# XCiT attention and a GELU MLP on one core: a rearranged start, the last stores in a fixed order, a fourth output buffer, six more Strassen sets and a new step order

## The chip, the core and the metric

The kernel runs on one core of a Trainium2 chip. Five engines work side by side, each through its own instructions in their written order: TensorE (PE in the profile; its weight loads are PEld), VectorE (DVE), ScalarE (ACT), GpSimd (POOL) and SyncE (SP). SP, ACT and POOL also issue DMA transfers. The metric is the device time of one execution in microseconds (us). Before the change the median of three runs is 684.43 us (683.51 to 684.55).

## The reference

For each of 4 batches, q, k and v are 6080 x 256. The columns of q and k are normalised over the tokens, a 256 x 256 attention matrix is taken over the channels, and v times that matrix goes through a two-layer MLP of width 2048:

```python
qn = q / (np.linalg.norm(q, axis=1, keepdims=True) + 1e-06)
kn = k / (np.linalg.norm(k, axis=1, keepdims=True) + 1e-06)
s = kn.transpose(0, 2, 1) @ qn / tau
a = np.exp(s - s.max(-1, keepdims=True)); a /= a.sum(-1, keepdims=True) + 1e-09
x = (v @ a).reshape(24320, 256)
h = x @ w_in
g = 0.5 * h * (1.0 + np.tanh(c * (h + 0.044715 * h * h * h)))
out = g @ w_out
```

## The kernel before

The kernel never forms `v @ a`. For each batch it computes `aw = a @ w_in` (256 x 2048, in four slices of 512 columns) and then `h` straight from the transposed tokens `vT` and `aw`. The tokens are cut into 25 blocks: 0 to 5, 6 to 11 and 12 to 17 belong to the first three batches (five blocks of 1024 tokens and one of 960 each), 18 to 24 to the last (five of 1024, one of 512, one of 448; block 24 is `LAST`).

Start (batch 0). The chunks of q and k are loaded by DMA; for each, `early_squares` squares q on ACT and k on DVE, `gram_row` adds k against q into the bank `G` (two matmuls of 256 columns a row), and `ss_rows` sums the squares through matmuls with ones (`SS[1]` for k, 256 columns wide; `SS[0]` for q, one column). The first four chunks are folded on DVE from eight rows to four (`early_fold`), the last two are not. The last chunk arrives in five pieces. `warm` issues matmuls on zeros. `scores` then takes roots by `Ln` and `Exp` on ACT (`lnk`, `rk`, `lnq`, `rq`), scales `G` on DVE into `S`, and takes the exponentials into `eT` (two halves). `pe_vt` transposes the first 512 tokens on PE and `pe_vt_copy` copies them to `vT`. `first_aw` sums the rows of `eT`, takes the reciprocal `rs` and makes the first slice of `aw` in four pieces, three copied on DVE and one on ACT. After that the first product of the MLP can run.

Body. All steps of all blocks stand in one text, `ORDER`, whose words are run in turn; so the text fixes the order on each engine. A word names a step, its part, the PSUM bank it opens (`@a` to `@g`, and `@z`) and the block or batch. The first product of the MLP comes in two forms. A plain step (`g.u_x`, then `G.u_x`) is two 512-column matmuls and a GELU on ACT. A set replaces four plain steps by seven products (`m1` to `m7`) after Strassen and Winograd, with two copies on ACT (`wcq`, `wy5`; `Y5_DVE` may send the second to DVE), two additions on DVE (`wap`, `wax`) and four GELUs (`wGp`, `wGs`, `wGr`, `wGx`). A full block has seven sets and four plain steps; blocks 0, 1, 2, 6, 7, 8, 12, 13 and 14 have fewer sets, 150 in all. The second product uses the same scheme for blocks 0 to 23 (`M1` to `M7` with token sums `T1` to `T4`). `T3`, which `M7` reads, is done for blocks 1 to 22 by an accumulating DMA issued on POOL (`token_sum`). Block 24 uses plain products (`D`, in `direct`), each over all channels of both output halves, into one bank for each half of the tokens.

While a batch runs, the next one's q and k are loaded, squared, folded and summed, so DVE and ACT have work of two kinds. Each result bank is turned by a DVE transpose into an output buffer `ot` (pool `yout`, three buffers), of which `store` issues four DMA stores, on SP. For block 24 the words `sB` and `sA` place the stores of its two halves within the order, alternating SP and ACT. In the built program the transfers issued by SP and ACT count their landing on eight counters in turn.

Of the kernel before, what the change touches and what calls it, by code (L numbers as in the profile page):

```python
# [16 lines left out]
def kernel(  # L17
# [46 lines left out]
    yout = ctx.enter_context(tc.tile_pool(name="yout", bufs=3))  # L64
# [180 lines left out]

    def ss_rows(c, which, rows=None):
# [28 lines left out]
    def scores(b):  # L275
        lnk = smx.tile([128, 256], FP32, tag="lnk")
        nc.scalar.activation(lnk, SS[1], AF.Ln, bias=eps)
        rk = smx.tile([128, 256], FP32, tag="rk")
        nc.scalar.activation(rk, lnk, AF.Exp, scale=-0.5)
        lnq = smx.tile([128, 2], FP32, tag="lnq")  # L280
        nc.scalar.activation(lnq, SS[0], AF.Ln, bias=eps)
        rq = smx.tile([128, 2], FP32, tag="rq")
        nc.scalar.activation(rq, lnq, AF.Exp, scale=-0.5, bias=log_it)
        S = smx.tile([128, 2, 256], FP32, tag="S")
        eT = smx.tile([128, 2, 256], BF16, tag="eT")
        for jc in range(2):
            nc.vector.tensor_mul(S[:, jc, :], G[b][:, jc, :], rk)
        for jc in range(2):
            nc.scalar.activation(eT[:, jc, :], S[:, jc, :], AF.Exp, scale=rq[:, jc : jc + 1])
        ET[b] = eT  # L290
# [15 lines left out]
    def k_row(b):  # L306
        rr, rh = NRM[b]
        dg = smx.tile([128, 256], FP32, tag="lnk", name=f"dg{b}")
# [155 lines left out]
    def pe_vt_copy(n, h, cc):  # L464
        x, y = parts_of(n)[h]
        nc.vector.tensor_copy(vt_tile(n)[:, cc, x:y], VPS[n, h][:, cc, :])
# [218 lines left out]
    def token_sum(n, i, h):  # L685

        hc = hc_of(n)
        if i == 3:
            o = quarter(n, 0, 1, h)
        else:  # L690
            o = tp.tile([128, 4, 512], BF16, tag="tx" if i in (1, 4) else "ty", name=f"t{i}{h}_{n}")[:, :, :hc]
        TS[n, i, h] = o
        if i == 3 and n in SUMS_DMA:
# [34 lines left out]
    def direct(n, p, t, tag):  # L728

        hc = hc_of(n)  # L730
        for m in range(2):
            first = (n, t) not in ACC
            if first:
                ACC[n, t] = bank(tag, [128, 512], f"o{n}_{t}")
                BITS[tag] = 2 * hc
            for fc in (2 * p, 2 * p + 1):
                w = ((A11, A12), (A21, A22))[m][fc // 8]
                mm(ACC[n, t][:, m * hc : m * hc + hc], lhsT=wcomb[:, w, fc % 8, :],
# [3 lines left out]
    XS, CS, OT, TURNED = {}, {}, {}, {}  # L742
# [11 lines left out]
    def store(n, tj, engines):  # L754
# [5 lines left out]
        for bi in range(4):  # L760
            engines[bi].dma_start(
                out=dst[bi],
                in_=ot[bi * 32 : bi * 32 + 32, 0 : hc // 32].rearrange("p x h c -> p x (h c)"))

    def mm2_step(n, what, tag):
# [13 lines left out]
        elif what in ("sA", "sB"):  # L779
            store(n, 1 if what == "sA" else 0, (nc.sync, nc.scalar, nc.sync, nc.scalar))  # L780
        else:
            ci, tj = {"c22": (1, 1), "c11": (0, 0), "c12": (0, 1), "c21": (1, 0)}[what]
            if n == LAST:
                src = ACC[n, tj][:, ci * hc : ci * hc + hc]
# [6 lines left out]
    with tc.manual_schedule():  # L791
# [29 lines left out]
        for c in range(nch - 1):  # L821
# [41 lines left out]
        warm(8)  # L863
# [3 lines left out]
        pe_vt_copy(0, 0, 1)  # L867
# [72 lines left out]


# [11 lines left out]
Y5_DVE = {}  # L953
# [3 lines left out]
g.3_0@f:0 g.0_0@g:0 g.2_0@a:0 aw.2@b:0 aw.3@c:0 ac.2:0 ac.3:0 g.1_0@d:0 vp.1@z:0 vc.1_1:0 vc.1_0:0  # L957
g.7_0@e:0 aw.5@b:0 ac.5:0 G.7_0:0 aw.4@c:0 G.2_0:0 g.5_0@e:0 ac.4:0 aw.7@a:0 ac.7:0 lk.0:1 g.4_0@b:0
G.1_0:0 G.0_0:0 G.5_0:0 G.3_0:0 g.3_1@d:0 G.3_1:0 g.10_1@g:0 g.2_1@c:0 aw.6@e:0 g.9_0@a:0 g.1_1@f:0
lk.1:1 SW.0:0 g.4_1@d:0 G.4_0:0 G.10_1:0 G.9_0:0 g.5_1@b:0 pA21:0 G.2_1:0 ac.6:0 g.14_1@g:0 G.1_1:0  # L960
vp.0@z:1 g.12_1@e:0 g.11_1@a:0 g.10_0@c:0 pA11:0 pS3:0 vc.0_0:1 G.5_1:0 g.6_1@f:0 G.11_1:0 G.4_1:0
G.14_1:0 G.10_0:0 g.8_0@b:0 G.12_1:0 lq.0:1 g.0_1@a:0 g.9_1@d:0 g.15_1@g:0 g.6_0@c:0 g.8_1@e:0
G.0_1:0 G.9_1:0 pF0:0 g.7_1@a:0 lv.1:1 G.6_0:0 G.6_1:0 G.8_1:0 vc.0_1:1 g.13_1@d:0 G.7_1:0 G.13_1:0
pS1:0 SW.1:0 pF1:0 T1.1:0 T1.0:0 pS4:0 M1.1@c:0 g.3_0@f:1 G.15_1:0 g.4_0@e:1 pNA:0 G.4_0:1 lq.1:1
g.15_0@a:0 G.3_0:1 g.12_0@d:1 g.0_0@g:1 M1.0:0 g.11_0@e:0 G.8_0:0 lt.1:1 T2.0:0 g.10_0@f:1 T3.1:0
pA12:0 G.11_0:0 G.12_0:1 G.10_0:1 ksq.0:1 M5.1@b:0 M5.0:0 lv.0:2 y5:0 G.15_0:0 qsq.0:1 row.0_2@z:1
T2.1:0 g.13_0@e:0 f1.0:1 row.0_1:1 row.0_4:1 g.2_0@d:1 g.14_0@f:0 m1.1@b:1 G.0_0:1 G.2_0:1 pS2:0
f2.0:1 vs:1 lq.2:1 g.12_0@a:0 f3.0:1 T3.0:0 g.8_0@g:1 G.14_0:0 G.12_0:0 wcq.1@d:1 row.0_3:1 G.8_0:1
# [12 lines left out]
m5.3@e:2 m2.3:2 G.0_0:2 row.2_5:1 y5:1 T2.0:1 wy5.3:2 G.4_0:2 wy5.1:2 row.2_2:1 m1.1@f:2 m6.3:2
T3.1:1 g.12_0@a:2 row.3_5:1 g.8_1@e:2 row.2_1:1 row.3_0:1 wap.3@c:2 wcq.1@b:2 m6.1:2 row.3_4:1
G.8_1:2 lq.5:1 wap.1@e:2 G.12_0:2 m2.1:2 wGp.3:2 f2.3:1 m7.3:2 row.3_3:1 m3.3:2 wax.3:2 row.2_4:1
M1.0@a:1 m5.2@g:2 m3.1:2 m7.1:2 M1.1:1 gc:1 wGs.3:2 f3.3:1 T4.0:1 lv.1:3 m1.5@c:2 sp.3@z:1 m4.3:2
wGx.3:2 wGp.1:2 wy5.2:2 wGs.1:2 g.12_1@b:2 T3.0:1 wax.1:2 cq@g:1 ksq.4:1 qsq.4:1 m4.1:2 M2.1:1
wGr.3:2 wcq.5@e:2 G.12_1:2 wGr.1:2 m1.2@d:2 m2.5:2 wcq.2@b:2 M2.0:1 m5.5@f:2 lq.6:1 sa.3:1 f1.4:1
m6.2:2 m2.2:2 wGp.5:2 m1.6@e:2 M6.0:1 m6.5:2 wy5.5:2 wcq.6@f:2 lk.6:1 c11:1 wGp.2:2 f2.4:1 wap.2@a:2
T4.1:1 m3.2:2 m7.2:2 m2.6:2 wGx.1:2 wax.2:2 g.0_1@b:2 M6.1:1 wGs.2:2 m4.2:2 wGp.6:2 G.0_1:2
wap.5@a:2 f3.4:1 m6.6:2 ap@f:1 c22:0 wGr.2:2 wGx.2:2 m5.6@b:2 m3.5:2 lt.0:3 sp.4@z:1 ksq.5:1 m7.5:2
m1.7@d:2 M7.1:1 wax.5:2 qsq.5:1 f1.5:1 sa.4:1 f2.5:1 lt.1:3 M3.1:1 M7.0:1 m4.5:2 wGs.5:2 wcq.7@a:2  # L990
wy5.6:2 M3.0:1 m6.7:2 ax:1 m5.7@b:2 f3.5:1 wGr.5:2 wy5.7:2 m2.7:2 sp.5@z:1 M4.0:1 wGx.5:2 wap.6@c:2
sa.5:1 m7.6:2 wap.7@b:2 wax.6:2 qsq.6:1 wGp.7:2 row.4_2@z:1 row.4_3:1 m3.7:2 m7.7:2 c12:1 ksq.6:1
# [342 lines left out]
```

## Time and profile before

| | us |
|---|---|
| median of three runs | 684.43 (683.51 to 684.55) |
| the profiled execution's own time | 684.09 |
| its span in the trace | 682.3 |
| first product of the MLP starts | 38.23 |
| last matmul ends | 675.7 |
| last transpose of the output ends | 676.5 |

The page gives busy time and share for each engine, the span in 40 slices, and the chain of work that ended last, followed back from the end. Start times are counted from the start of the span. A row of the timeline reads: start, duration, engine, line, operation, output and inputs, shapes, count, and in brackets the idle time before it and what ended it. Rows of groups end in total busy time, mean nanoseconds of one, idle time before, and its causes. Matmuls overlap, so a matmul's duration in a row is longer than the time until the next one starts. ACTq, SPq and POOLq are the issuing sides of those engines.

### The profile page before, as it was taken

The page shows a single profiled execution, that of the slowest core. Times are in us where ns is not written, and L with a number is a line of the kernel's source. Part 1 is how long each engine was busy: PE and PEld are TensorE (multiplying, and loading weights), DVE is VectorE, ACT ScalarE, POOL GpSimd, SP SyncE. Part 2 cuts the span into 40 slices and gives each one's busy share as a digit, 9 for nine tenths or more (in the row PEclk, how much of TensorE's full clock was granted, in tenths as well). Part 3 has the DMA queues.
Part 4 walks back from the last instruction along what each step waited for, and adds up shares of the span by engine and source line. Part 5 has one row for each costly group of instructions (what it writes and reads, how often), then busy time and mean ns, then how long its engine had stood idle before and what let it go on. Part 6 is the DMA issues. An engine that isn't in the chain of part 4 may idle for free.

```text
span 682.3 us, 10610 instructions
## 1 busy us (share of the span) xinstructions
PE 663.0 (97%) x3579; PEld 336.3 (49%) x3579; DVE 612.2 (90%) x941; ACT 621.5 (91%) x1193; POOL 112.4 (16%) x177
## 2 busy tenths in 40 slices
PE   3999999999999999999999999999999999999996
PEld 2855455454445454554444444545444444444575
DVE  3579999999998999999999999989998988888893
ACT  5379999899999998999989999999999999999982
POOL 4321121121120121103101111202011011101100
PEclk9999999999999999999999999999999999999999
DMA  9998999998989999959779999878386587558445
GB/s 240 208 256 126 151 180 167 178 165 136 175 151 175 171 164 155 175 80 166 129 135 169 175 167 197 134 134 150 69 148 115 101 151 147 101 107 152 81 84 96
DMA packets 168807, 101.70 MB, mean 149 GB/s; under 512 B 150240, under 2 KB 153952, under 8 KB 168032
## 3 DMA queue, kind: packets, MB, share of 16 engines
q0 software_dynamic: 20688, 62.34, 53.2%
q1 hardware_dynamic: 146816, 37.41, 29.6%
q10 hardware_dynamic: 1248, 1.28, 0.6%
q8 instruction: 28, 0.46, 0.3%
q14 instruction: 27, 0.22, 0.1%
HBM read 78.91 MB, written 36.57 MB: 169 GB/s over the span
## 4 chain that ended last, share of the span: by engine, by line
PE 93%; DMA 3%; DVE 2%; ACT 0%; issue 0%; SPq 0%; POOL 0%; DVEq 0%; POOLq 0%
PE rb L481 18%; PE p L481 17%; PE q L481 15%; PE r L481 11%; PE h L481 10%; PE m L481 10%; PE G L205 6%; PE awp L375 2%; DMA qk_f<-in_q_dram 1%; DMA g<-g 1%; PE o L481 1%; PE warm L269 1%; PE ss L263 1%; DVE t L700 0%; DMA vT<-vb 0%; DVE q L622 0%
## 5 line engine op out<-in xcount | busy, mean ns | idle before, releaser
L481 PEld LDWEIGHTS <-wcomb 128*128 128x128 bf16 x1408 | 136.6, 98 | 144.9 <-issue 3.4
L631 ACT ACTIVATE g<-q 128x512 bf16<-128x512 f32 (+1 forms) x286 | 169.4, 623 | 5.7 <-PE q L481 5.1
L481 PEld LDWEIGHTS <-aw 128*128 128x128 bf16 x807 | 77.9, 98 | 77.1 <-DVE aw L415 1.3
L622 DVE TENSOR_TENSOR q<-rb,yw 128x512 f32<-128x512 f32 (+2 forms) x150 | 102.4, 687 | 13.3 <-PE rb L481 4.4
L700 DVE TENSOR_TENSOR t<-g,t 128x2048 bf16<-128x2048 bf16 (+2 forms) x96 | 112.7, 1180 | 0.1
L625 DVE TENSOR_TENSOR xw<-rb,yw 128x512 f32<-128x512 f32 (+2 forms) x150 | 101.5, 678 | 10.1 <-PE rb L481 7.5
L481 PE MATMUL rb<-tv,sw 128*128 128x512 bf16 (+3 forms) x314 | 109.2, 367 | 0.0
L539 ACT ACTIVATE g<-h 128x512 bf16<-128x512 f32 (+1 forms) x164 | 97.1, 650 | 5.3 <-PE h L481 5.1
L619 ACT ACTIVATE yw<-m 128x512 f32<-128x512 f32 (+2 forms) x150 | 93.0, 626 | 3.9 <-PE m L481 2.9
L481 PE MATMUL p<-t,wcomb 128*128 128x512 bf16 (+2 forms) x384 | 95.5, 373 | 0.0
L631 ACT ACTIVATE g<-xw 128x512 bf16<-128x512 f32 (+1 forms) x143 | 92.6, 650 | 2.7 <-DVE xw L625 2.3
L613 ACT ACTIVATE q<-rb 128x512 f32<-128x512 f32 (+2 forms) x150 | 90.6, 614 | 4.7 <-PE rb L481 3.0
L481 PE MATMUL r<-g,wcomb 128*128 128x512 bf16 (+2 forms) x384 | 94.7, 373 | 0.0
L481 PE MATMUL h<-vT,aw 128*128 128x512 bf16 (+2 forms) x336 | 93.5, 377 | 0.8 <-DVE aw L415 0.8
L481 PEld LDWEIGHTS <-sw 128*128 128x128 bf16 x628 | 61.2, 98 | 61.8 <-issue 1.2
L631 ACT ACTIVATE g<-rb 128x512 bf16<-128x512 f32 (+1 forms) x143 | 87.7, 619 | 2.5 <-PE rb L481 2.1
L694 POOL DMA_DIRECT2D g<-g x44 | 39.7, 917 | 196.3 <-ACT g L631 92.0
L700 DVE TENSOR_TENSOR t<-g 128x2048 bf16<-128x2048 bf16 (+2 forms) x48 | 56.4, 1184 | 1.6 <-ACT g L539 1.3
L481 PE MATMUL q<-vT,sw 128*128 128x512 bf16 (+3 forms) x157 | 56.2, 367 | 0.0
L481 PE MATMUL q<-vT,aw 128*128 128x512 bf16 (+3 forms) x157 | 55.8, 367 | 0.0
L481 PE MATMUL rb<-vT,aw 128*128 128x512 bf16 (+3 forms) x157 | 55.7, 367 | 0.0
L481 PE MATMUL m<-tv,sw 128*128 128x512 bf16 (+3 forms) x157 | 55.7, 367 | 0.0
(148 smaller groups left out, 858.4 us busy)
## 6 DMA issues: line engine op xcount, KB each, us to landing
out_dram<-ot SPq DMA_DIRECT2D x160, 128.0 KB, 4.3
g<-g POOLq DMA_DIRECT2D x38, 512.0 KB, 6.4
vb<-in_v_dram POOLq DMA_DIRECT2D x38, 256.0 KB, 5.2
k<-in_k_dram POOLq DMA_DIRECT2D x21, 384.0 KB, 5.6
q<-in_q_dram POOLq DMA_DIRECT2D x21, 384.0 KB, 5.8
g<-g POOLq DMA_DIRECT2D x6, 480.0 KB, 6.6
out_dram<-ot SPq DMA_DIRECT2D x24, 120.0 KB, 7.5
wst<-in_moe_w_out_dram POOLq DMA_DIRECT2D x2, 1024.0 KB, 10.4
```

The costliest lines, as they stand in the source:

```text
L205: nc.tensor.matmul(G[b][:, jc, :], lhsT=qt[:np_, r, jc * 128 : jc * 128 + 128], rhs=kt[:np_, r, :], start=first and jc == 0, stop=jc == 1, ...
L263: nc.tensor.matmul(SS[1], lhsT=ones_bf, rhs=sq[:, 256:512], start=c == 0 and r == 0, stop=end)
L375: nc.tensor.matmul(ps, lhsT=ET[b][:, jc, ic * 128 : ic * 128 + 128], rhs=win_bf[:, jc, fs * 512 : fs * 512 + 512], start=jc == 0, stop=jc ...
L481: GATE[0] = nc.tensor.matmul(*a, skip_group_check=True, **kw)
L539: nc.scalar.activation(g_half(n, u // 8)[:, x, u % 8], hp[:, :hc], AF.Gelu_apprx_tanh)
L613: nc.scalar.activation(Q[n, i, 0][:, :w], RB[n, i][:, :w], AF.Copy)
L619: nc.scalar.activation(YW[n, i][:, :w], M5.pop((n, i))[:, :w], AF.Copy)
L622: nc.vector.tensor_add(Q[n, i, 1][:, :w], RB[n, i][:, :w], YW[n, i][:, :w])
L625: nc.vector.tensor_add(XW[n, i][:, :w], RB[n, i][:, :w], YW.pop((n, i))[:, :w])
L631: nc.scalar.activation(g[:, t, k0], x[:, :w], AF.Gelu_apprx_tanh)
L694: nc.gpsimd.dma_start(out=o, in_=quarter(n, 1, 1, h), accum_op=ALU.add)
L700: (nc.vector.tensor_add if add else nc.vector.tensor_sub)(o, a, b)
```

## The change

The start is rearranged. The squares of k in the fifth chunk are folded on DVE (`early_fold_k`), as are two pairs of rows of q in the last chunk, so `ss_rows` sums four rows of k and two rows of q fewer. The last sums of q stand ahead of the last row of `G`. `warm(8)` becomes `warm(6)`. One of the two copies into `vT` goes to ACT.

Blocks 6, 7, 8, 12, 13 and 14 get a seventh set in place of four plain steps (156 sets in all, and 24 plain steps fewer). In blocks 18 to 22 two of the seven `y5` copies go to DVE. The whole `ORDER` is new, 3994 words for 3946.

In block 24 the second token half accumulates its two output halves in separate banks (`D.p_1_m`), so that 16 words become 24 for the same matmuls. The words `sA` and `sB` are gone: both halves are stored behind all steps, ACT and SP alternating, and a dependence that only fixes the order ties each store to the one before it. The pool `yout` has four buffers; `lnk`, `rk` and `dg` share the buffers of `dn` and `th`. A DMA form of `T2` is added to the code, for no block (`SUMS2_DMA` is empty).

In all, PE has 16 matmuls fewer: six of 512 columns in the body, and at the start six of 256 columns and four of one. DVE has 25 instructions more.

```diff
-    yout = ctx.enter_context(tc.tile_pool(name="yout", bufs=3))
+    yout = ctx.enter_context(tc.tile_pool(name="yout", bufs=4))
...
+    def early_fold_k(c):
+        k = [x[:, :, 256:512] for x in SQ[c]]
+        nc.vector.tensor_add(k[0], k[0], k[1])
...
-        lnk = smx.tile([128, 256], FP32, tag="lnk")
+        lnk = smx.tile([128, 256], FP32, tag="dn", name="lnk")
...
-    def pe_vt_copy(n, h, cc):
+    def pe_vt_copy(n, h, cc, eng="dve"):
         x, y = parts_of(n)[h]
-        nc.vector.tensor_copy(vt_tile(n)[:, cc, x:y], VPS[n, h][:, cc, :])
+        o, i = vt_tile(n)[:, cc, x:y], VPS[n, h][:, cc, :]
+        if eng == "act":
+            nc.scalar.activation(o, i, AF.Copy)
+        else:
+            nc.vector.tensor_copy(o, i)
...
-    def direct(n, p, t, tag):
+    def direct(n, p, t, *mt):
...
+        *ms, tag = mt
+        key = (n, t, *ms)
+        for m in ms or range(2):
+            first = key not in ACC
...
         for bi in range(4):
-            engines[bi].dma_start(
+            inst = engines[bi].dma_start(
                 out=dst[bi],
                 in_=ot[bi * 32 : bi * 32 + 32, 0 : hc // 32].rearrange("p x h c -> p x (h c)"))
+            if n == LAST:
+                tc.add_manual_dep(inst.ins, STORED[-1].ins.name, mybir.DependencyInfo(
+                    mybir.DependencyClass.NoSync, mybir.DependencyReason.SCHED_ONLY), reason="order")
+            STORED.append(inst)
...
-        elif what in ("sA", "sB"):
-            store(n, 1 if what == "sA" else 0, (nc.sync, nc.scalar, nc.sync, nc.scalar))
...
             if c < nch - 2:
                 early_fold(c)
+            else:
+                early_fold_k(c)
...
-        ss_rows(c - 1, 1)
+        ss_rows(c - 1, 1, range(0, 4))
         ss_rows(c - 1, 0)
         early_squares(c, 0, 0, 4, "act")
+        nc.vector.tensor_add(SQ[c][0][:, 0:2, 0:256], SQ[c][0][:, 0:2, 0:256], SQ[c][0][:, 2:4, 0:256])
         early_squares(c, 1, 0, 5, "dve")
         for i in range(4):
             gram_row(0, c, i)
-        ss_rows(c, 0, range(0, 4))
+        early_squares(c, 1, 5, 8, "dve")
         ss_rows(c, 1, range(0, 5))
-        early_squares(c, 1, 5, 8, "dve")
+        ss_rows(c, 1, range(5, 8))
         early_squares(c, 0, 4, 6, "dve")
-        ss_rows(c, 1, range(5, 8))
         for i in (4, 5):
             gram_row(0, c, i)
-        ss_rows(c, 0, range(4, 6))
+        ss_rows(c, 0, (0, 1, 4, 5))
         early_squares(c, 0, 6, 8, "dve")
-        for i in (6, 7):
-            gram_row(0, c, i)
-        ss_rows(c, 0, range(6, 8))
+        gram_row(0, c, 6)
+        ss_rows(c, 0, (6, 7))
+        gram_row(0, c, 7)
...
-        warm(8)
+        warm(6)
         pe_vt(0, 0, "e")
         scores(0)
         pe_vt_copy(0, 0, 0)
-        pe_vt_copy(0, 0, 1)
+        pe_vt_copy(0, 0, 1, "act")
...
+    for tj in range(2):
+        store(LAST, tj, (nc.scalar, nc.sync) * 2)
...
-Y5_DVE = {}
+Y5_DVE = {(18, 2), (18, 5), (19, 2), (19, 5), (20, 2), (20, 5), (21, 2), (21, 5), (22, 2), (22, 5)}
...
 ORDER = """
...
-D.2_0:24 wGx.3:24 wGr.2:24 D.6_1:24 D.0_0:24 wGs.2:24 D.7_0:24 D.1_0:24 D.6_0:24 D.2_1:24 D.5_1:24
-D.7_1:24 c11:24 c21:24 c12:24 sB:24 c22:24 sA:24
...
+D.0_1_1@d:24 D.5_1_1:24 D.1_0:24 m4.3:24 wGp.3:24 wGr.3:24 D.2_0:24 c21:23 D.3_0:24 c22:23 D.6_0:24
+wGx.3:24 wGx.2:24 D.7_0:24 D.7_1_0:24 c11:24 c21:24 D.1_1_1:24 D.2_1_0:24 D.5_1_0:24 wGs.3:24
+D.4_1_1:24 D.6_1_1:24 D.1_1_0:24 D.4_1_0:24 D.6_1_0:24 D.2_1_1:24 D.3_1_0:24 D.7_1_1:24 D.3_1_1:24
+c12:24 c22:24
```

More of the change, by code (lines that the diff above doesn't have):

```diff
@@ L307, in k_row @@
         rr, rh = NRM[b]
-        dg = smx.tile([128, 256], FP32, tag="lnk", name=f"dg{b}")
+        dg = smx.tile([128, 256], FP32, tag="dn", name=f"dg{b}")
         for ic in range(2):
@@ new lines @@
+wy5.1:13 row.0_5:3 wcq.2@g:13 lt.1:14 M4.1:11 m1.3@b:13 T3.0:12 wy5.2:13 m2.2:13 row.1_4:3 m6.2:13
+wap.1@c:13 m3.1:13 wcq.3@e:13 c21:11 wGx.7:12 wGp.2:13 row.1_0:3 m2.3:13 m7.1:13 row.1_2:3 m5.3@d:13
+T1.1:12 wGp.3:13 wax.1:13 wGs.1:13 T3.1:12 M5.0@g:12 M5.1:12 m6.3:13 gc:3 wap.2@e:13 m3.2:13 m4.1:13
+wGx.1:13 wy5.3:13 lv.1:15 lk.4:3 y5:12 wGr.1:13 wGs.2:13 g.0_0@c:13 g.8_0@d:13 G.0_0:13 m7.2:13
+G.8_0:13 T2.1:12 T2.0:12 wax.2:13 sp.1@z:3 m5.5@g:13 m1.5@f:13 M1.1@e:12 wy5.5:13 M1.0:12 wap.3@c:13
```

701 lines of the change are left out of this document (352 added, 349 removed).

## The prediction

> **What bounds the kernel now.** I read the page first (span, busy shares, the slices with the granted clock), then the chain of waits, then busy time by stage, and last the timeline of the two ends.
>
> ```profile
> span 682.3 us, 10610 instructions
> PE 663.0 (97%) x3579; PEld 336.3 (49%) x3579; DVE 612.2 (90%) x941; ACT 621.5 (91%) x1193; POOL 112.4 (16%) x177
> PEclk9999999999999999999999999999999999999999
> PE 93%; DMA 3%; DVE 2%; ACT 0%; issue 0%; SPq 0%; POOL 0%; DVEq 0%; POOLq 0%
> ```
>
> TensorE works at its full granted clock in every slice and carries 93% of the chain that ended last. Because overlapping matmuls make a busy PE look fuller than it is, I check by stage:
>
> ```profile
> 0.00:38.20 38.20, 26.25 (x250) 20.42 (x250) 18.34 (x38) 17.51 (x23) 16.68 (x31) 1.00 1.07 222
> 38.20:180.00 141.80, 141.09 (x744) 69.20 (x745) 135.07 (x209) 133.24 (x254) 26.91 (x44) 1.00 0.95 170
> 180.00:340.00 160.00, 159.96 (x828) 77.76 (x827) 153.27 (x237) 154.65 (x301) 28.00 (x42) 1.00 0.87 152
> 340.00:500.00 160.00, 160.00 (x827) 78.08 (x826) 152.58 (x235) 153.25 (x296) 26.01 (x40) 1.00 0.87 149
> 500.00:671.70 171.70, 171.70 (x896) 87.10 (x894) 151.49 (x222) 161.28 (x322) 14.76 (x20) 1.00 0.66 118
> 671.70:676.50 4.80, 4.02 (x42) 3.77 (x40) 1.43 (x4) 1.53 (x4) 0.00 (x0) 1.00 0.40 66
> 676.50:682.30 5.80, 0.00 (x0) 0.00 (x0) 0.00 (x0) 0.00 (x0) 0.00 (x0) 0.71 0.44 74
> ```
>
> The columns are the stretch, its length, then busy time of PE, weight loads, DVE, ACT and POOL. From 38.2 to 671.7 us PE idles 0.75 us in all, so in the body time changes only through the number of matmuls or through new stalls. Two stretches are open: 38.2 us before the first product of the MLP, and 5.8 us behind the last matmul, in which no engine computes. DVE (95 to 96% in three stages) and ACT (94 to 97%) stand close behind PE; this is what speaks against the change.
>
> **The change part by part.**
>
> *Six more sets.* Blocks 6, 7, 8, 12, 13 and 14 go from six sets to seven. A set of seven 512-column products replaces four plain steps of two each, so six matmuls disappear. One costs, in the chain of waits:
>
> ```profile
> 48.74 5.18 PE h L481 x24
> ```
>
> 5.18 / 24 = 0.216 us, so 6 x 0.216 = 1.3 us less on the engine that sets the time. In return each set adds two DVE additions and two ACT copies (its four Gelus replace the plain ones):
>
> ```profile
> L622 DVE TENSOR_TENSOR q<-rb,yw 128x512 f32<-128x512 f32 x126 | 86.8, 693 | 11.1 <-PE rb L481 3.6 <-ACT yw L619 3.3 <-ACT g L631 1.5
> L625 DVE TENSOR_TENSOR xw<-rb,yw 128x512 f32<-128x512 f32 x126 | 85.9, 683 | 8.6 <-PE rb L481 5.9 <-ACT g L631 1.1 <-ACT g L539 0.3
> L619 ACT ACTIVATE yw<-m 128x512 f32<-128x512 f32 x126 | 78.9, 634 | 3.6 <-PE m L481 2.9 <-DVE sv L193 0.3
> L613 ACT ACTIVATE q<-rb 128x512 f32<-128x512 f32 x126 | 76.9, 622 | 3.4 <-PE rb L481 2.1 <-ACT yw L619 0.2
> 42.24 2.07 ACT L539 ACTIVATE g<-h 128x512 bf16<-128x512 f32 x4 [3.19 <-PE h L481]
> ```
>
> Busy time over count: DVE 86.8/126 + 85.9/126 = 1.37 us a set, ACT 78.9/126 + 76.9/126 = 1.24 us. Three sets fall into each of the stages 180 to 340 and 340 to 500: DVE 153.3 + 4.1 = 157.4 and ACT 154.7 + 3.7 = 158.4 of about 159.4 us. That is nearly full, but the row of four Gelus takes 2.07 us, 0.52 each, against the 0.62 that the rows above average over the run: operations that stand back to back overlap, so a stage 99% busy by this measure still has room. In blocks 18 to 22, ten copies `y5` go from ACT to DVE, priced by the nearest row (0.68 us, also 512 columns out of PSUM): 6.8 us into a stage where DVE has 20 us free. Nothing on the path, as long as DVE keeps that room.
>
> *The new order.* Every step is placed anew. The chain of waits shows the one long stall of the body, which the second row puts down:
>
> ```profile
> 122.48 8.76 DMA g<-g
> 131.28 1.02 PE p L481 x4
>   PE p L481: 0.7, 1
> DMA to landing us min/median/max: 6.3/7.5/8.8
> ```
>
> (The last two rows are of the accumulating transfers' own view around 100 to 135 us: who waited, and their landing.) In block 2 of the old order 43 matmuls stand between the second of these transfers and the product that reads it, in the new one 55, some 2.6 us more, over the 0.7 us waited. So -0.7 (bounds 0 and -0.7: the landing may grow too). Against that I set +0.8 for waits that the fuller DVE and ACT bring; below it is 0, as in the last full-seven stage, where PE idles 0.00; above I take 3, for rival 3. POOL issues the same transfers, only earlier or later; its 16% busy covers that.
>
> *Start.* The rows, in time:
>
> ```profile
> 31.70 1.90 DVE L160 TENSOR_TENSOR sq<-qk_g1b 128x1024 bf16<-128x1024 bf16 x4 [1.63 <-DMA qk_g1b<-in_k_dram]
> 32.89 1.03 PE L263 MATMUL ss<-sq,ones_bf 128*128 128x256 bf16 x8
> 33.93 0.43 DVE L160 TENSOR_TENSOR sq<-qk_g1b 128x512 bf16<-128x512 bf16 x1 [0.33 <-DMA qk_g1b<-in_q_dram]
> 34.30 0.60 PE L205 MATMUL G<-qk_g1b 128*128 128x256 bf16 x4
> 34.73 0.24 PE L257 MATMUL ss<-ones_bf,sq 128*128 128x1 bf16 x4
> 34.83 1.03 PE L269 MATMUL warm<-zeros_bf,ones_bf 128*128 128x256 bf16 x8
> 35.00 0.76 DVE L287 TENSOR_TENSOR S<-G,rk 128x256 f32<-128x256 f32 x2 [0.64 <-PE ss L257]
> 35.01 0.26 ACT L281 ACTIVATE lnq<-ss,eps 128x2 f32<-128x2 f32 x1
> 35.63 0.91 ACT L289 ACTIVATE eT<-S,rq 128x256 bf16<-128x256 f32 x2
> 36.35 0.76 DVE L466 COPY vT<-vt_ps 128x512 bf16<-128x512 bf16 x2 [0.59 <-PE vt_ps L461]
> 36.59 0.20 PE L402 MATMUL sums<-ones_bf,eT 128*128 128x1 bf16 x2
> 37.02 0.16 DVE L405 RECIPROCAL rs<-sums 128x2 f32<-128x2 f32 x1
> 37.28 0.47 ACT L413 ACTIVATE aw<-aw_ps,rs 128x256 bf16<-128x256 f32 x1 [0.74 <-DVE rs L405]
> ```
>
> The last squares end at 33.93 + 0.43 = 34.36, held by their load, and that stays. Behind them PE has a queue: two rows of G before the last `ss`, because eight row sums occupy it from 32.89. The folds take four k sums and two pairs of q sums off PE, and the last `ss` moves ahead of the last row of G: it can end at 34.36 + 0.24 = 34.6 where it ended at 34.97, and `lnq` starts 0.35 us sooner. `S` needs the whole of G and stays near 35.0, so `eT` starts at about 35.0 + 0.38 + 0.03 = 35.4, 0.2 sooner. Then the reciprocal: today it stands behind both copies of vT (to 37.11), though its sums end at 36.79. With the second copy on ACT, which idles 0.74 us there, and two warm matmuls fewer, it follows the sums, themselves 0.2 sooner: about 36.6. Gain 0.4 us. Bounds: 0.1, if the weights' load for the next products (issued as PE is still summing) is what is late next, and 0.5. The two folds lie in DVE's 1.63 us wait ahead of 31.70; without that cover they would cost about 1 us. Sharing the buffers of `lnk`, `rk` and `dg`, and a fourth output buffer, cost nothing: their next users stand far behind.
>
> *End.*
>
> ```profile
> 671.73 4.00 PE L481 MATMUL o<-g,wcomb 128*128 128x224 bf16 x40
> 675.76 0.71 DVE L748 STREAM_TRANSPOSE ot<-o 128x224 f32<-128x224 f32 x2 [0.44 <-PE o L481]
> 675.75 1.68 ACTq L761 DMA_DIRECT2D out_dram<-ot  x3
> 677.62 2.02 SPq L761 DMA_DIRECT2D out_dram<-ot  x4
> SPq L761 <- DMA out_dram<-ot: 3.3, 1, 3.3
> DMA to landing us min/median/max: 1.7/1.8/1.9
> ```
>
> Each store counts its landing on one of eight counters taken in turn, and waits until that counter's former store has landed. Today SP's first store of the last block shares its counter with the ACT store issued at 675.75, whose landing (about +1.8) is 677.6: SP waits 3.3 us and issues its four until 679.6. In the fixed order the eight last stores have eight counters. The last transposes also read two banks, so the first runs under the last four matmuls: one is left behind PE, 0.3 us gained. But the stores of block 23 now come late, all eight on SP just ahead. The product that frees them has 52 matmuls behind it (52 x 4.00/40 = 5.2 us), two transposes take 0.7, and an issue takes 2.02/4 = 0.5: SP is busy with them from about 4.4 us before PE's end for 4.0, then issues two of block 24, then the last two, which must also wait for landings of block 23. I get the last issue 1.0 to 1.9 us behind PE's end, landing 1.8 later: 2.8 to 3.7 us behind it, against 679.64 - 0.5 + 1.8 - 675.73 = 5.2 now. Gain 1.5 to 2.4; I take 2.1, nearer the upper end, since the issues have their row and only the landings' overlap is unknown.
>
> The Trainium skill ("DMA: Bandwidth & Descriptors", section "Issuing engines are not separate DMA queues") says that transfers issued from several engines share the same 16 DMA engines, and that more issuing engines save only issue time. By that rule reordering the stores gains nothing but the 0.3 us of the transposes, and the sum would be 682.5. The SP row above speaks against it: the wait is of the issuer, not of the transfer.
>
> *Sum* against the profiled execution's 684.09 us (span 682.3 and 1.8 around it): -1.3 - 0.7 + 0.8 - 0.4 - 2.1 = -3.7, giving 680.4; the median of the three runs is 0.3 above that execution, so 680.7.
>
> **Rivals.**
>
> 1. *The stores gain nothing*: something other than the counters holds them, or SP's eight stores of block 23 push them back. For: SP's queue is full from before PE's end. Against: the 3.3 us row. 682.5.
> 2. *DVE or ACT becomes the bound* in blocks 6 to 8 and 12 to 14 (slower). One mechanism: once DVE's queue fills, each added addition delays the Gelu that frees a bank, and PE waits for it one for one. It decides when the stages pass 100%, 2 us from the 157.4 above. Price 6 x 1.37 = 8.2 us, the 1.3 not gained and 0.8 not counted twice: 684.4 - 0.7 - 0.4 - 2.1 + 8.2 = 689.4. Against: overlap.
> 3. *The new order is looser*: a few dozen short waits of 0.1 us at steps set too close, 3 us in all; the body's idle 0.75 us shows how little of this the old one has. 680.7 + 2.2 = 682.9, or 683.6 with the transfer's stall still there.
>
> **How the numbers follow.** Forecast 0.70, rival 1 0.12, rival 2 0.06, rival 3 0.12. About 0.2% (1.4 us) is what a measurement of this kernel can tell from no change: faster is below 683.1, slower above 685.8. Faster holds the forecast, rival 1 and a third of rival 3: 0.86; same the rest of rival 3: 0.08; slower 0.06. The range 679.5 to 682.9 takes the forecast's bounds (best: 684.4 - 1.3 - 0.7 - 0.5 - 2.4 = 679.5) and reaches to rival 1 and the lower of rival 3.
>
> **What would show it.** Start: the first `h` near 37.8 us instead of 38.2, with the reciprocal right behind the sums. Body: 3563 matmuls instead of 3579, PE idle under 1.5 us from the first `h` on, no long `g<-g` piece in the chain. End: SP waiting for DVE, not for a store, and the span ending 4 to 5 us behind the last matmul instead of 6.6. Wrong if DVE or ACT takes over the chain in mid-kernel, or if the last landing stays 5 us behind PE.

## The result, and the profile after

The changed kernel takes 681.06 us (median of six runs, 680.50 to 681.83) beside 684.49 us for the kernel before (six runs, 683.51 to 687.16): ratio 0.9945, 95% interval 0.9927 to 0.9963. A second set of runs gave 681.69 beside 684.08 us, ratio 0.9963 (0.9951 to 0.9976). Both say faster by more than 0.2%; the predicted 680.7 is 0.4 and 1.0 us below the two medians.

The page of the changed kernel, with the rows that stand against those of before (span, then busy time and share with the number of instructions, and the granted clock):

```profile
span 680.0 us, 10558 instructions
PE 656.9 (97%) x3502; PEld 334.7 (49%) x3563; DVE 624.7 (92%) x964; ACT 624.9 (92%) x1196; POOL 113.1 (17%) x177
PEclk9999999999999999999999999999999999999998
```

The weight loads count 3563, as predicted (DVE has 23 instructions more in the pages, 964 for 941, not the 25 of the section on the change); 61 matmul records are missing from this trace (PE x3502), so PE's idle time can't be read from it. A second profiled execution of the same kernel has all 3563. Its chain of waits by engine (also without the missing records), and what PE waited for from the first product on:

```profile
span 679.3 us, 10619 instructions
PE 88%; ACT 5%; DMA 4%; DVE 1%; issue 1%; POOL 0%; DVEq 0%; ACTq 0%; POOLq 0%
```

```profile
PE h L489 <- DVE aw L419: 0.6, 1, 0.6
```

The wait of 0.6 belongs to the start. ACT now has 5% of the chain, where it had none: at some points the work that ended last ran through ACT, without PE idling there. The stages (length, then busy time of PE, weight loads, DVE, ACT and POOL):

```profile
37.70:180.00 142.30, 142.24 (x750) 69.83 (x751) 136.32 (x212) 135.84 (x259) 27.12 (x45) 1.00 0.98 169
180.00:340.00 160.00, 159.90 (x827) 77.88 (x826) 156.45 (x243) 157.30 (x306) 28.00 (x42) 1.00 0.91 156
340.00:500.00 160.00, 159.89 (x826) 77.69 (x825) 155.86 (x241) 156.59 (x305) 27.01 (x42) 1.00 0.87 147
500.00:669.00 169.00, 169.00 (x882) 85.77 (x881) 155.08 (x229) 154.82 (x304) 14.12 (x19) 1.00 0.65 117
673.70:679.30 5.60, 0.00 (x0) 0.00 (x0) 0.04 (x1) 0.00 (x0) 0.00 (x0) 0.65 0.57 103
```

From the first product to 669 us PE idles 0.06 + 0.10 + 0.11 = 0.27 us, against 0.75 in the old order, although DVE and ACT are fuller. The last row is the stretch behind the last transpose: 5.6 us in which nothing computes, against 5.8 before. That stretch is where the prediction expected the largest gain.

To see where the time came from, I cut each trace at two weight loads on PE, that of the first product of the MLP and the last one of all. (The last matmul starts 0.1 us behind the latter.) All figures are us of the profiled execution; the last column is the median less that of the kernel before, timed beside it on the same chip (684.49 in the first row of the changed kernel; else 684.10, 683.68 or 684.08).

| kernel | first load | first to last load | last landing behind last load | median, less before |
|---|---|---|---|---|
| before | 38.23 | 637.14 | 5.61 | |
| changed | 37.80 | 635.33 | 5.22 | 681.06, -3.4 |
| changed, second set | 37.75 | 635.18 | 4.71 | 681.69, -2.4 |
| `before_end` | 37.83 | 637.05 | 4.03 | 681.89, -1.8 |
| `old_body` | 37.71 | 638.13 | 4.00 | 682.76, -1.3 |
| `old_start` | 38.41 | 634.97 | 4.94 | 681.32, -2.8 |
| `free_order` | 37.47 | 635.18 | 6.99 | 683.49, -0.6 |
| `split23` | 37.98 | 635.19 | 4.29 | 680.88, -3.2 |
| `early22` | 37.70 | 635.46 | 3.36 | 679.86, -3.8 |
| `early22_again` | 37.94 | 635.47 | 3.43 | 680.39, -3.7 |
| `three_out` | 37.84 | 635.70 | 4.28 | 681.81, -2.3 |
| `dve_one` | 37.76 | 638.15 | 4.64 | 684.13, +0.5 |
| `dve_three` | 37.66 | 645.45 | 5.14 | 691.82, +8.1 |
| `y5_act` | 37.76 | 640.54 | 5.57 | 687.03, +3.0 |

By this table the first load came 0.4 to 0.5 us sooner, the body was 1.8 to 2.0 shorter, the end 0.4 to 0.9. The start of the changed kernel, as its timeline shows it:

```profile
33.80 0.43 DVE L160 TENSOR_TENSOR sq<-qk_g1b 128x512 bf16<-128x512 bf16 x1 [0.27 <-DMA qk_g1b<-in_q_dram]
34.28 0.25 PE L261 MATMUL ss<-ones_bf,sq 128*128 128x1 bf16 x4
34.57 0.26 ACT L285 ACTIVATE lnq<-ss,eps 128x2 f32<-128x2 f32 x1
35.40 0.91 ACT L293 ACTIVATE eT<-S,rq 128x256 bf16<-128x256 f32 x2 [0.24 <-DVE S L291]
36.36 0.20 PE L406 MATMUL sums<-ones_bf,eT 128*128 128x1 bf16 x2
36.60 0.17 DVE L409 RECIPROCAL rs<-sums 128x2 f32<-128x2 f32 x1 [0.26 <-PE sums L406]
36.86 0.47 ACT L417 ACTIVATE aw<-aw_ps,rs 128x256 bf16<-128x256 f32 x1
```

From the start of the last squares to the first copy of `aw` it takes 36.86 - 33.80 = 3.06 us, where it took 37.28 - 33.93 = 3.35. So the change gives 0.3, and the other 0.1 is a landing of q that came sooner. The other runs bear this out: the interval is 3.06 or 3.07 us in every trace with the new start, and 3.40 and 3.45 in the two other traces with the old one (`before_end`, `old_start`), while the first load itself moves with that landing, in `before_end` to 37.83 with the old start. The reciprocal stands right behind the sums (36.56).

The end, from DVE's, ACT's and SP's timelines:

```profile
669.01 0.40 DVE L765 STREAM_TRANSPOSE ot<-c 128x256 f32<-128x256 f32 x1
671.04 0.71 DVE L765 STREAM_TRANSPOSE ot<-o 128x224 f32<-128x224 f32 x2 [1.62 <-PE o L489]
673.14 0.80 DVE L765 STREAM_TRANSPOSE ot<-o 128x224 f32<-128x224 f32 x2 [1.40 <-PE o L489]
669.12 1.83 SPq L778 DMA_DIRECT2D out_dram<-ot  x4
671.04 2.13 SPq L778 DMA_DIRECT2D out_dram<-ot  x1
673.23 1.47 SPq L778 DMA_DIRECT2D out_dram<-ot  x3
674.80 2.21 SPq L778 DMA_DIRECT2D out_dram<-ot  x4
671.78 0.36 ACTq L778 DMA_DIRECT2D out_dram<-ot  x1
673.84 1.14 ACTq L778 DMA_DIRECT2D out_dram<-ot  x2
674.65 1.50 ACTq L778 DMA_DIRECT2D out_dram<-ot  x2
```

(The third ACT row repeats the second's last store: the stretches asked for overlap.) SP issues the eight stores of block 23 from 669.12 to 674.70, one of them for 2.13 us, and only then its four of block 24. The transposes are where the prediction put them, one under the last matmuls, one behind. ACT has nothing to compute any more, yet its second store of block 24's first half, turned by 671.75, goes out at 673.84. In the built program it counts on the counter of the third store of block 23, which the view of the output stores shows by itself:

```profile
L778 SPq DMA_DIRECT2D out_dram<-ot x1: 468/468/468, 670.0 to 670.0; - x1
DMA to landing us min/median/max: 3.8/3.8/3.8
```

Issued at 669.97, landed 3.8 us later, at 673.8: that is what ACT waited for.

### The profile page after: what moved, and what is told of

The parts are those of the page before. It is cut to its first block, busy times and chain, and to the rows that moved or that the text cites. A ratio compares the mean times of both kernels' runs of the same rounds, so it can differ in the third digit from the quotient of the medians.

```text
span 680.0 us, 10558 instructions
## 1 busy us (share of the span) xinstructions
PE 656.9 (97%) x3502; PEld 334.7 (49%) x3563; DVE 624.7 (92%) x964; ACT 624.9 (92%) x1196; POOL 113.1 (17%) x177
## 4 chain that ended last, share of the span: by engine, by line
PE 81%; ACT 10%; DMA 4%; DVE 2%; issue 2%; POOL 0%; DVEq 0%; ACTq 0%; POOLq 0%
PE rb L489 17%; PE p L489 16%; PE q L489 14%; PE r L489 10%; PE m L489 9%; PE h L489 8%; ACT g L639 5%; PE G L205 4%; DMA qk_g1b<-in_k_dram 3%; PE awp L379 2%; ACT q L621 1%; DMA qk_g1a<-in_q_dram 1%; ACT yw L627 1%; PE o L489 1%; ACT sq L158 1%
## 5 line engine op out<-in xcount | busy, mean ns | idle before, releaser
L639 ACT ACTIVATE g<-q 128x512 bf16<-128x512 f32 (+1 forms) x298 | 178.6, 622 | 4.4 <-PE q L489 3.3
L630 DVE TENSOR_TENSOR q<-rb,yw 128x512 f32<-128x512 f32 (+2 forms) x156 | 106.2, 686 | 8.2 <-PE rb L489 3.5
L633 DVE TENSOR_TENSOR xw<-rb,yw 128x512 f32<-128x512 f32 (+2 forms) x156 | 105.0, 676 | 5.5 <-PE rb L489 4.6
L621 ACT ACTIVATE q<-rb 128x512 f32<-128x512 f32 (+2 forms) x156 | 95.1, 612 | 5.5 <-PE rb L489 4.1
L639 ACT ACTIVATE g<-xw 128x512 bf16<-128x512 f32 (+1 forms) x149 | 97.2, 655 | 0.6 <-DVE xw L633 0.4
L639 ACT ACTIVATE g<-rb 128x512 bf16<-128x512 f32 (+1 forms) x149 | 91.3, 620 | 2.1 <-PE rb L489 1.8
L627 ACT ACTIVATE yw<-m 128x512 f32<-128x512 f32 (+2 forms) x146 | 90.2, 623 | 2.7 <-PE m L489 1.8
L547 ACT ACTIVATE g<-h 128x512 bf16<-128x512 f32 (+1 forms) x140 | 81.8, 630 | 4.8 <-PE h L489 4.4
L489 PE MATMUL h<-vT,aw 128*128 128x512 bf16 (+2 forms) x277 | 77.4, 377 | 1.2 <-DVE aw L419 1.0
L489 PE MATMUL rb<-tv,aw 128*128 128x512 bf16 (+3 forms) x160 | 57.0, 367 | 0.2
```

Source lines behind the costliest of these rows:

```text
L489: GATE[0] = nc.tensor.matmul(*a, skip_group_check=True, **kw)
L547: nc.scalar.activation(g_half(n, u // 8)[:, x, u % 8], hp[:, :hc], AF.Gelu_apprx_tanh)
L621: nc.scalar.activation(Q[n, i, 0][:, :w], RB[n, i][:, :w], AF.Copy)
L627: nc.scalar.activation(YW[n, i][:, :w], M5.pop((n, i))[:, :w], AF.Copy)
L630: nc.vector.tensor_add(Q[n, i, 1][:, :w], RB[n, i][:, :w], YW[n, i][:, :w])
L633: nc.vector.tensor_add(XW[n, i][:, :w], RB[n, i][:, :w], YW.pop((n, i))[:, :w])
```

## The experiments

Theory A was that block 23's stores, which the new order frees late, push the last stores back; its rival, that the end is held by the DMA engines, whoever issues.

**`split23`.** Block 23's second half is stored behind all steps, ACT and SP alternating.

```diff
-        if TURNED[n, tj] == 2 and n != LAST:
+        if TURNED[n, tj] == 2 and n != LAST and (n, tj) != (LAST - 1, 1):
...
+    store(LAST - 1, 1, (nc.scalar, nc.sync) * 2)
     for tj in range(2):
         store(LAST, tj, (nc.scalar, nc.sync) * 2)
```

> Against the changed kernel's 681.1 us. The four stores of block 23's second half are taken out of SP's queue and put behind all steps, ACT and SP alternating, ahead of the last eight, which stay as they are. Nothing else changes. Theory A (SP's eight late stores of block 23 push the last ones back: in the changed kernel SP issues them from 669.1 to 674.7, and each of the last eight waits for the landing of one of them on its counter, 674.58 to 676.48): the last issue comes about 1.5 us sooner, 1.2 to 1.7 us behind PE's end instead of 3.2 to 3.7, and the time is 679.5 (679.2 to 680.0). Rival B (the DMA engines hold the end, whoever issues): within 0.3 us of 681.1, with landings as late as before.

680.88 us: the time is not 679.5 but within the 0.3 us of 681.1 that the rival allowed. Yet the last landing came 0.4 to 0.9 us sooner behind the last load than in the changed kernel's two executions, which the rival did not expect. Taken alone this is inconclusive: the stores still stand just ahead of block 24's, only on two queues.

**`early22`.** One word moves, so that four of the eight stores leave 5 to 7 us earlier.

```diff
-wGs.2:24 ax:23 m7.2:24
+wGs.2:24 ax:23 c22:23 m7.2:24
...
-c21:23 D.3_0:24 c22:23 D.6_0:24
+c21:23 D.3_0:24 D.6_0:24
```

(Parts of two lines of `ORDER`.)

> Against the changed kernel's 681.1 us (span 680.0, last landing 678.35, in its profiled execution). One word moves: the last transpose of block 23's second half stands right behind the addition that it reads, in a gap of DVE at 665.4, instead of behind three more steps at 669.0. Its four stores then leave SP from about 665.9 on, and those of the first half from 669.1 to 671.0, so SP is free before block 24's first half is turned at 671.75. Theory A (block 23's late stores hold the last eight): last issue near 675.0, last landing 676.6 to 677.2, time 679.5 to 680.2. Rival B (after the split of these stores over two engines moved the last landing by 0.9 but the median by only 0.2 to 0.3: landings, not issues, hold the end): 680.7 to 681.1.

> The kernel with block 23's second half turned and stored early, beside the changed kernel on the same chip. Theory A (block 23's late stores cost the changed kernel 1.2 at its end): 1.0 to 1.5 us below the changed kernel of this call. If the two earlier medians, 679.86 and 681.06, differed by the chip alone: within 0.4.

679.86 us, and beside the changed kernel on one chip 680.39 (680.18 to 680.52) against 681.69 (681.05 to 682.37): 1.3 us faster, without overlap. Ratio to before 0.9943 (0.9931 to 0.9956). SP and ACT at the end of the second execution:

```profile
672.05 2.06 SPq L778 DMA_DIRECT2D out_dram<-ot  x2
674.24 0.92 SPq L778 DMA_DIRECT2D out_dram<-ot  x2
674.25 0.93 ACTq L778 DMA_DIRECT2D out_dram<-ot  x2
673.42 0.80 DVE L765 STREAM_TRANSPOSE ot<-o 128x224 f32<-128x224 f32 x2 [1.40 <-PE o L489]
```

Now the last four stores follow the last transpose (673.42 + 0.80 = 674.22) at once on both engines. Theory A holds, and this version beats both kernels.

**`before_end`.** The kernel before, with its last eight stores behind all steps and in the fixed order, and nothing else.

```diff
-D.7_1:24 c11:24 c21:24 c12:24 sB:24 c22:24 sA:24
+D.7_1:24 c11:24 c21:24 c12:24 c22:24
...
+    for tj in range(2):
+        store(LAST, tj, (nc.scalar, nc.sync) * 2)
```

> The kernel before with one thing changed: the last eight stores behind all steps, ACT and SP alternating, in a fixed order. Theory A (in the old step order block 23's stores are issued by 674.3, so the fixed order is worth what the prediction took, about 2): last landing 3.5 to 4 us behind the last matmul instead of 5.4, time 684.1 - 1.5 to 2.0 = 682.1 to 682.6. Rival B (stores gain nothing): 684.1. Body waits as in the kernel before, with the accumulating transfer's landing from 0 to 0.8 late.

681.89 against 683.68 us, ratio 0.9971 (0.9961 to 0.9981): storing so gives 1.8 us in the old step order. The last landing moves from 5.61 to 4.03 behind the last load. SP's and ACT's rows:

```profile
674.86 2.04 SPq L761 DMA_DIRECT2D out_dram<-ot  x4
674.87 2.10 ACTq L761 DMA_DIRECT2D out_dram<-ot  x4
```

SP starts its four stores of the last block as soon as they are turned, where it waited 3.3 us for a landing before.

**`free_order`.** The changed kernel without the dependence that fixes the order.

```diff
-            if n == LAST:
-                tc.add_manual_dep(inst.ins, STORED[-1].ins.name, mybir.DependencyInfo(
-                    mybir.DependencyClass.NoSync, mybir.DependencyReason.SCHED_ONLY), reason="order")
-            STORED.append(inst)
```

> Against the changed kernel's 681.1 us. The dependence that fixes the order of the last eight stores is left out; ACT and SP still alternate and stand behind all steps. In the built program ACT's last stores then take counters 0, 5 and 7 ahead of SP's, and SP's first store of block 24 shares counter 5 with an ACT store of the second half. Theory A (the counter sharing costs what the prediction took from the 3.3 us row): SP waits for that landing, about 1.8 us behind an issue at 674.0, and issues its four from 675.8 on, so the last landing is about 679.3 instead of 678.35 and the time 682.0 (681.6 to 682.8). Rival B (the order is worth nothing, the stores are held by SP's queue or by the DMA engines either way): 681.1, within 0.3.

683.49 us, more than expected. SP's waits and its timeline:

```profile
SPq L778 <- DMA out_dram<-ot: 3.9, 2, 3.6
```

```profile
668.63 0.81 SPq L778 DMA_DIRECT2D out_dram<-ot  x2
673.03 5.26 SPq L778 DMA_DIRECT2D out_dram<-ot  x10
```

The mechanism is the expected one, a landing on a shared counter, but it strikes sooner: SP's third store of block 23 waits 3.6 us for ACT's first one of block 24, and then ten issues in a row, this one the first, take 5.26 us. In the new order the fixed order is therefore worth 1.8 to 2.8 (-0.6 against -2.4 and -3.4), and without it the end is 1.4 us worse than before (6.99 against 5.61).

**`old_body`.** The changed kernel's code with the old step order (150 sets, `Y5_DVE` empty).

```diff
-Y5_DVE = {(18, 2), (18, 5), (19, 2), (19, 5), (20, 2), (20, 5), (21, 2), (21, 5), (22, 2), (22, 5)}
+Y5_DVE = {}
...
-                src = ACC[n, tj, ci] if tj else ACC[n, tj][:, ci * hc : ci * hc + hc]
+                src = ACC[n, tj, ci] if (n, tj, ci) in ACC else ACC[n, tj][:, ci * hc : ci * hc + hc]
...
```

(`ORDER` goes back as a whole, without `sA` and `sB`.)

> The changed kernel's code with the old step order, 150 sets and no second copies on DVE (start, fixed last stores and four output buffers as changed). Theory A (start 0.4 and, as block 23's stores are out of SP's queue by 674.3 in this order, the full 2.0 at the end; the body is where the new order gains 1.3 of matmuls and the 0.7 of the transfer): 684.5 - 0.4 - 2.0 = 682.1 (681.8 to 682.8), first h near 37.8, 637.3 us from the first h to PE's end against 635.5 in the changed kernel, the g<-g stall still there, last landing 3.3 to 4 us behind PE's end. Rival B (the last stores gain nothing in any order): 683.9 to 684.2.

682.76 us (681.80 to 685.52), within the expected range, though the ratio to before, 0.9988 (0.9977 to 0.9998), leaves anything from 0.1 to 1.6 us. In the profiled execution the end is as expected (4.00), but the body is 1.0 us longer than that of the kernel before, and the expected g<-g stall is missing. Two landings differ. First the load that transposes block 1's tokens, here and then in the kernel before (the view of `vT`, 57 to 65 us):

```profile
DMA to landing us min/median/max: 6.8/6.8/6.8
```

```profile
DMA to landing us min/median/max: 5.0/5.0/5.0
```

Then the weight load that waits for it here, and the second accumulating transfer of block 2, also here (the view of `g`):

```profile
64.33 0.11 PEld L489 LDWEIGHTS <-aw 128*128 128x128 bf16 x2 [1.21 <-DMA vT<-vb]
```

```profile
DMA to landing us min/median/max: 7.5/7.5/7.5
```

PE loses 1.2 us to a transfer that took 6.8 instead of 5.0, and does not lose the 0.7 of the g<-g stall, since that transfer took 7.5 instead of 8.8. Three more shifts of 0.1 to 0.3 us, near 182, 244 and 557, I have not traced.

**`old_start`.** The changed kernel with the old start.

```diff
-            else:
-                early_fold_k(c)
...
-        warm(6)
+        warm(8)
...
-        pe_vt_copy(0, 0, 1, "act")
+        pe_vt_copy(0, 0, 1)
```

(The order of the sums and squares in the last chunk goes back too.)

> The changed kernel with the old start (no folds in the last two chunks, old order of the sums, eight warm matmuls, both copies into vT on DVE). Theory A (the start gains 0.3 to 0.4): 681.5 (681.3 to 681.7), first h near 38.2. Rival B (the load of the weights for the next products is what is late, 0.1): 681.1 to 681.2, first h below 37.95.

681.32 us, between the two medians of the changed kernel, so its time decides nothing. The trace does: 37.47 - 34.02 = 3.45 us from the last squares to the first copy of `aw`, against 3.06. The first load is 0.6 us later than in the changed kernel's first execution, the last load only 0.24 later: the body took up the rest.

**`dve_one`, `dve_three`.** One or three more copies a block go from ACT to DVE in the six blocks with a new set.

```diff
-Y5_DVE = {(18, 2), (18, 5),
+Y5_DVE = {(6, 3), (7, 3), (8, 3), (12, 3), (13, 3), (14, 3), (18, 2), (18, 5),
```

(The start of the line; the rest stays. `dve_three`: sets 3, 5 and 6 of the same blocks.)

> The changed kernel with one copy y5 a block moved from ACT to DVE in the six blocks that got a seventh set: DVE gets 3 x 0.68 = 2.0 us more in each of the stages 180 to 340 and 340 to 500, where it is busy 156.4 and 155.8 of 160. Theory A (a stage that is 98% busy by this measure still has room, since operations standing back to back overlap): 681.1 to 681.5. Rival (DVE is at its bound, each addition delays the Gelus one for one): 2.0 a stage, less what idle it has, at least 682.5.

> The same with three copies a block: 9 x 0.68 = 6.1 us more in each of the two stages, which would make 162.5 and 161.9 of 160. Theory A (overlap leaves some room, but not 6 us): a loss of 1 to 4 us, 682 to 685, with PE waiting for Gelus whose input DVE makes. Rival (DVE was at its bound already): 6.1 twice, 12 us, 693.

684.13 and 691.82 us: theory A fell. Against 635.3, the mean of the changed kernel's two bodies, they are 2.9 and 10.2 us longer, 0.48 and 0.57 us a copy. Stage 180 to 340 with one copy, then with three, and PE's longest waits in 180 to 500 with three:

```profile
180.00:340.00 160.00, 158.97 (x820) 77.10 (x819) 156.52 (x243) 154.77 (x300) 27.22 (x41) 1.00 0.90 153
```

```profile
180.00:340.00 160.00, 155.59 (x801) 75.27 (x800) 156.07 (x244) 148.65 (x286) 25.33 (x38) 1.00 0.87 148
```

```profile
PE rb L489 <- DVE q L630: 3.1, 7, 0.8
PE rb L489 <- DVE yw L625: 1.1, 1, 1.1
```

DVE's busy time stays at the 156.4 of the changed kernel (156.5 and 156.1) however much it is given; PE waits for DVE's products instead.

**`y5_act`.** The ten copies of blocks 18 to 22 go back to ACT.

```diff
-Y5_DVE = {(18, 2), (18, 5), (19, 2), (19, 5), (20, 2), (20, 5), (21, 2), (21, 5), (22, 2), (22, 5)}
+Y5_DVE = {}
```

> The changed kernel with the ten copies y5 of blocks 18 to 22 back on ACT, which gets 10 x 0.62 = 6.2 us more in 500 to 669, where it is busy 155.1 of 169; DVE gets 6.8 less. The prediction priced this part at nothing because that stage has room. If ACT has room too: 680.9 to 681.4. If the stage's room is only apparent (in the other stages DVE's busy time stood still at 156.5 of 160 when it was given more): ACT at 161 of 169 is where the old order had it, so a loss of at most 1, 681.4 to 682.0.

687.03 us: both expectations missed. The body is 5.2 us longer, 0.52 a copy, with this stage:

```profile
500.00:669.00 169.00, 166.48 (x831) 80.59 (x829) 145.25 (x211) 156.62 (x309) 14.16 (x19) 1.00 0.63 115
```

51 matmuls fewer fit into the stretch (831 for 882; those at its end are shorter than 512 columns), and yet ACT is busy for 93% of it and DVE for 86%. ACT was busier than that in the old order (161.28 of 171.70, 94%) and PE idled 0.00. A shorter piece says the same. From 595 to 620 us, here and then in the kernel before:

```profile
595.00:620.00 25.00, 23.83 (x108) 10.52 (x108) 19.04 (x27) 23.24 (x47) 2.78 (x4) 1.00 0.57 104
```

```profile
595.00:620.00 25.00, 25.00 (x117) 11.32 (x116) 21.88 (x32) 24.71 (x50) 3.58 (x5) 1.00 0.62 112
```

So the busy share of ACT does not account for the loss. What fits is the order: each step stands where its neighbours' durations let it stand, and one operation more on ACT (0.62 us) delays what is behind it almost one for one (0.52). That is inferred; no run varied the places of these steps alone.

The Trainium skill ("Perfetto Trace Analysis", section "Identifying the Most-Contended Engine") takes the occupancy of the Vector and Scalar engines as a fair measure of how near they are to their limit. As a measure of the room left in this written order it does not hold: the body grew by 5.2 us with ACT at 93% and DVE at 86%, and did not with ACT at 94% in the old order.

**`three_out`.** Three output buffers again; the order on every engine is the same.

```diff
-    yout = ctx.enter_context(tc.tile_pool(name="yout", bufs=4))
+    yout = ctx.enter_context(tc.tile_pool(name="yout", bufs=3))
```

> The changed kernel with three output buffers instead of four; the order on every engine is the same. If the fourth buffer costs and gains nothing, as the prediction has it: 680.9 to 681.2. If the late stores of block 23 make block 24's first transpose wait for a buffer: its output is the fourth behind block 22's second half, whose stores are issued some 8 us ahead, so at most 0.5 more. If DVE, which stands at its bound, waits for buffers in the body: 682 or more.

> The changed kernel itself, beside the other three on the same chip: 680.9 to 681.2.

681.81 beside 681.69 us: the fourth buffer changes nothing that can be measured in the time. (Both lie about half a microsecond above the 680.9 to 681.2 that was expected of them from the first set of runs.) The trace does show it. With three buffers the last two transposes wait 2.3 us, until a store of block 23 has landed; they start 0.9 us behind the last load, where they start with it in the changed kernel (at most 0.5 was expected), and both run behind the last matmul:

```profile
674.46 0.71 DVE L765 STREAM_TRANSPOSE ot<-o 128x224 f32<-128x224 f32 x2 [2.31 <-DMA out_dram<-ot]
```

Yet the last landing is 4.28 us behind the last load, no later than with four buffers (5.22 and 4.71): there the transposes were done sooner, but the stores waited for landings anyway. What the fourth buffer is worth once block 23 is stored early, as in `early22`, no run shows.

## Why the prediction came out, point by point

**The sum.** That the time came out near 680.7 is in part luck: two errors of opposite sign, the end 1.2 to 1.7 us short of its gain and the body 0.6 to 0.8 better, cancel in part, and the rest, 0.7 to 1.4 us in the profiled executions, stays within the range. Against the first profiled execution (span 682.3 to 680.0) and the second (679.3) the terms are:

| term | predicted | measured |
|---|---|---|
| six products and the body's waits | -1.3 - 0.7 + 0.8 = -1.2 | -1.8, -2.0 |
| start, to the first load | -0.4 | -0.4, -0.5 (0.3 of it the change's own) |
| end, to the last landing | -2.1 | -0.4, -0.9 |
| behind the last landing | 0 | +0.3, +0.3 |

(From the last landing to the end of the span it is 682.31 - 680.98 = 1.33 us before, 1.63 after; the cause is open.)

**The end failed.** The step was "I get the last issue 1.0 to 1.9 us behind PE's end, landing 1.8 later". The last issue came 3.0 and 2.5 us behind it, and the span ended 6.5 and 6.0 us behind the last matmul, not the 4 to 5 that were to show the gain. The step put SP's eight stores of block 23 at 4.0 us; they took 5.6, one issue lasting 2.13 us for an assumed 0.5, and landings took up to 3.8 us for 1.8, on which block 24's stores waited through the counters. The profile before had such a store already, outside the rows that the prediction used: SP's at 671.90 took 1.38 us to issue and 2.8 to land. So the first rival, stores pushed back by SP's eight of block 23, held to a large part. That the fixed order itself is worth about 2 was right: `before_end` shows 1.8, `free_order` 1.8 to 2.8. What the prediction mis-sized is what the new order takes away again by turning block 23 late, 1.3 us (`early22`). With that undone the last landing is 3.4 us behind the last load and 3.0 to 3.1 behind PE's end, inside the predicted 2.8 to 3.7.

**Rival 1's rule.** The Trainium skill ("DMA: Bandwidth & Descriptors", section "Issuing engines are not separate DMA queues") says that starting transfers from several engines saves issue time only. In `before_end` the same two engines issue the same stores, and 1.8 us are gained, because an issuer no longer waits for another's landing. The rule leaves that wait out.

**The body was better than forecast.** New waits were set at +0.8. PE's idle time fell from 0.75 to 0.27 us instead; the long g<-g wait is gone although its transfer took 8.3 us:

```profile
L707 POOL DMA_DIRECT2D g<-g x1: 966/966/966, 122.7 to 122.7; - x1
DMA to landing us min/median/max: 8.3/8.3/8.3
```

It lands at 131.0, and the product that reads it starts only at 132.95, by its place in the order:

```profile
132.95 1.03 PE L489 MATMUL p<-g,wcomb 128*128 128x512 bf16 x4
```

(The prediction gives 43 and 55 matmuls between the transfer and its reader; by start times the traces have 40 in the kernel before and 53 in the second execution, the same difference within one.) The 0.7 is not a fixed price: in the old order `before_end` shows the stall again (0.6 us, a landing of 8.7), but in `old_body` the same transfer at the same distance landed in time. How much of the body's gain is the six sets' and how much the new order's, no run separates: `old_body` takes both back.

**The margin of DVE and ACT was misread.** The prediction held that a stage 99% busy still has room because operations overlap, and that the second rival decides only 2 us beyond 157.4. DVE came out at 156.4. `dve_one` shows that the next 2.0 us a stage, up to 158.4 of 160, cost 2.9 in all. Rival 2 did not happen, but it stood right behind the change, not 2 us away. Whether DVE is at its own limit there or the order at its, the runs leave open; `y5_act` points to the order, since there the loss comes with neither engine as busy as that. The copies priced at "nothing on the path" are worth 5.2 us in this order, though undoing one part of an order that was made with it is no measure of that part in the old one.

**Start.** Right by its steps: `lnq` at 34.57 for 35.01, `eT` at 35.40 as forecast, the reciprocal behind the sums. Rival 3 did not happen.

## What to carry to other kernels

Price a store by where it stands in its issuer's queue and by whose landing its counter waits for, not by its own issue time; and look at what is issued just ahead of the last stores, because a gain at the end is easily given back there. A busy share, whether 93% or 98%, did not tell here how much slack a written order has; moving a small known cost did, as one copy that cost 0.5 us. A stall on a landing in one profile is a draw from a spread (0.7, 0.6 and 0 us in three executions of one order here), so price it with the bound 0.

## What was unexpected of the hardware

Stores in a row do not all land alike. In the changed kernel's last 12 us the DMA engines' mean busy share and throughput, in 40 slices of 668 to 680 us, were

```profile
DMA  0000003876958003801969699899999590000000
GB/s 0 0 0 0 0 0 67 143 129 112 207 96 139 9 0 61 128 10 21 148 109 156 117 167 157 129 161 268 196 170 174 117 156 12 0 0 0 0 0 0
```

Between 671.9 and 673.4 the engines nearly stop twice while stores are outstanding; no store lands from 671.33 to 673.82 us. The same pause, 2.1 to 2.5 us, lies in the second execution (671.12 to 673.24) and in those of `before_end` (671.27 to 673.74) and `early22` (671.34 to 673.58). One store issue in it takes 2.13, 1.64 and 1.67 us in the first three, where others take about 0.45. The kernel before has the pause too (671.75 to 674.06), under stores of block 23 that did not hold its end. One thing coincides with it: in each of these traces one packet of 16 KB, of the DMA queue that the page calls instruction, starts within 0.3 us of the pause's begin (at 671.22 us in the changed kernel, lasting 1.5). But in `free_order`, where such a packet starts at 670.75, a store issued at 671.29 lands in 1.7 us. So what causes the pause stays open.
